# Where the attention mask is applied and who copies the state: VectorE, ScalarE and GpSimd in a chunked linear attention ahead of two feed-forward stages

## The chip, the cores and the metric

The kernel runs on one core of one Trainium2 chip. The metric is the device time of one execution in microseconds (us), lower is better. The engines are called as the profile calls them: PE is TensorE (PEld its weight loads), DVE is VectorE, ACT is ScalarE, POOL is GpSimd, SP is SyncE, which here only issues DMAs.

## The reference

Three stages follow each other. The first is a linear attention with decay, over 4 batches, 8 heads, 768 steps and a head dimension of 48:

```
for t in range(S):
    state = alpha[:, :, t, :, None] * state + np.einsum('bhd,bhe->bhde', k[:, :, t], v[:, :, t])
    y[:, :, t] = np.einsum('bhd,bhde->bhe', q[:, :, t], state)
```

Its output, 3072 tokens of 384 numbers, goes through a mixture of 8 experts with one expert for each token (384 to 1024 to 384, ReLU, scaled by two gates), and that through a dense stage (384 to 2048 to 384, squared ReLU). Everything is float32.

## The kernel before

The attention is done in 24 chunks of 128 steps, 6 for each batch. A chunk holds all 8 heads as 4 pairs (NP) of two halves a = 0 and 1; a half sits on partitions 64a to 64a + 47. For each chunk i:

- `decay(i)`: PE transposes alpha (`tr`, L268), ACT copies it out (`al`, L288, and its first column `a`, L291), DVE makes suffix and prefix products with two scans (`sp`, L294 and L303).
- `scaled(i)`: PE transposes k and q, and DVE multiplies them by the products as it takes them from PSUM (`kh`, `qh`, L318).
- `scores(i)`: PE multiplies `kh` with `qh` into two PSUM tiles `sc`, one for each half (L337). Then the causal mask is put on them: the tiles `m`. The two halves go different ways, and the change is here.
- `khat(i)` and `update(i)`: `kh` is transposed back (`khp`, L365), copied by ACT (`khn`, L367), and multiplied with v (`u`, L378). DVE adds the old state and multiplies by the decay (`st`, L383 or L385 and L387), and the new state is copied twice, once for each half, into the diagonal blocks of a zeroed tile `both` (L391). This copy is the other place of the change. It happens for chunks 0 to 4 of each batch, 20 times in all.
- `outputs(i)`: PE adds `both` times `qh` (L400) and `m` times v (L404) in PSUM tile `y`, ACT copies it to `yt` (L409).
- `rows(i)`, `logits(i)`: PE turns `yt` into token rows and gate logits (`fx`, L425), ACT copies the rows (`xn`, L435), DVE reduces the logits (`lg`, L442).

The chunks are pipelined by hand: iteration i of the loop at L770 writes out `scores(i+1)`, `scaled(i+2)`, `rows(i-1)`, `logits(i-1)`, `decay(i+3)`, `khat(i+1)`, `outputs(i)`, `update(i+1)`. So `m` and `both` of a chunk are needed by PE about one iteration after they are asked for. Every engine takes its instructions in the order written; waits are by semaphores.

Between these, small routing steps for groups of finished chunks are slipped into DVE's stream (`pulse`, a step or two at a time), and finished rows are scaled by ACT or DVE (`xn`, L574 and L572) and sent to their expert's place in memory by a scatter that POOL issues (`xs`, L129, after a tiny memset, L128). From chunk 19 on, the experts' weights are fetched and split in two parts by `parts`: ACT casts (L170), then POOL or, in the last iteration of the loop, DVE subtracts (both L171). The routing step `rk` (L503) of the last group of three chunks waits for DVE at the end of the attention. Behind that come the experts and the dense stage, which are matmuls of PE almost without a break.

Of the kernel before, what the change touches and what calls it, by code (L numbers as in the profile page):

```python
# [9 lines left out]
F32 = mybir.dt.float32  # L10
# [4 lines left out]
ALU = mybir.AluOpType  # L15
# [12 lines left out]
def moe_block_kernel(ctx: ExitStack, tc: tile.TileContext, q, k, v, alpha, w_gate, w_ogate,  # L28
                     w1, w2, w_in, w_out, out, dbg=None):
    nc = tc.nc  # L30
# [4 lines left out]
    P = 128  # L35
    NP = H // 2
# [29 lines left out]
    a1 = att.enter_context(tc.tile_pool(name="a1", bufs=1))  # L66

    with tc.manual_schedule():
# [7 lines left out]
        nc.scalar.activation(spare, ones[:, 0:1], AF.Exp)  # L76
        ident = const.tile([P, P], F32, name="ident")
        make_identity(nc, ident)
        mask = a1.tile([P, P], F32, name="mask")
        nc.gpsimd.memset(mask, 1.0)  # L80
        nc.gpsimd.affine_select(out=mask, in_=mask, pattern=[[1, P]], compare_op=ALU.is_ge,
                                fill=0.0, base=0, channel_multiplier=-1)
        tri = const.tile([P, P], BF16, name="tri")
        nc.gpsimd.memset(tri, 1.0)
        nc.gpsimd.affine_select(out=tri, in_=tri, pattern=[[1, P]], compare_op=ALU.is_gt,
                                fill=0.0, base=0, channel_multiplier=-1)
# [157 lines left out]
        both = []  # L244
# [85 lines left out]
        def scores(i):  # L330
            if i >= NCH:
                return
            ps = [p_sc.tile([P, NP, P], F32, tag="sc", name="sc") for _ in range(2)]
            for pr in range(NP):
                for a in range(2):
                    r = slice(64 * a, 64 * a + D)
                    nc.tensor.matmul(ps[a][:, pr, :], kh[i][r, pr, :], qh[i][r, pr, :],  # L337
                                     start=True, stop=True)

            held = [(gi, ranks(gi)) for gi in list(routing) if gi in waited or gi >= PICK - 1]  # L340
            waited.update(routing)
            for a in range(2):
                m = ms_p.tile([P, NP, P], F32, tag="m", name="m")
                if a == 0 and i > 0:
                    nc.vector.tensor_tensor(out=m, in0=ps[a],
                                            in1=mask.unsqueeze(1).to_broadcast([P, NP, P]),
                                            op=ALU.mult)
                else:
                    nc.scalar.copy(m, ps[a])
                    nc.gpsimd.affine_select(out=m, in_=m, pattern=[[0, NP], [1, P]],  # L350
                                            compare_op=ALU.is_ge, fill=0.0, base=0,
                                            channel_multiplier=-1)
                msk[i, a] = m
            for gi, ps in held:
                place(gi, ps)

        def has_next(i):
            return i < NCH and (i + 1) % NC != 0
# [11 lines left out]
        def update(i):  # L370
            if not has_next(i):
                return
            t = khn.pop(i)
            vt = slot("v", i)
            ps = p_1.tile([P, NP, D], F32, tag="ku", name="u")
            for pr in range(NP):
                for a in range(2):
                    nc.tensor.matmul(ps[64 * a:64 * a + 64, pr, :], t[:, pr, 64 * a:64 * a + 64],  # L378
                                     vt[:, 2 * pr + a, 0:D], start=True, stop=True)
            s = a3.tile([P, NP, D], F32, tag="st", name="st")  # L380
            pb = pend[i + 1].unsqueeze(2).to_broadcast([P, NP, D])
            if i % NC == 0:
                nc.vector.tensor_tensor(out=s, in0=ps, in1=pb, op=ALU.mult)  # L383
            else:
                nc.vector.tensor_tensor(out=s, in0=ps, in1=st[i], op=ALU.add)  # L385
                pulse()
                nc.vector.tensor_tensor(out=s, in0=s, in1=pb, op=ALU.mult)  # L387
            st[i + 1] = s
            for a in range(2):
                r = slice(64 * a, 64 * a + D)  # L390
                nc.scalar.copy(both[(i + 1) % 2][r, :, r], s[r])  # L391
            pulse()

        def outputs(i):
# [103 lines left out]
        def ranks(gi):  # L498
            n, g0 = GROUPS[gi], gstart[gi]
            s8 = [P, n, E]  # L500
            oh = onehot[:, g0:g0 + n, :]
            ps = psum(n)
            nc.tensor.matmul(ps, tri, oh, start=True, stop=False)  # L503
            nc.tensor.matmul(ps, ones, tot[:, gi:gi + 1, :].to_broadcast(s8), start=False,
                             stop=(n == 1))
            for c in range(n - 1):
                nc.tensor.matmul(ps[:, c + 1:, :], ones,
                                 oh[:, c:c + 1, :].to_broadcast([P, n - 1 - c, E]), start=False,
                                 stop=(c == n - 2))
            return ps  # L510
# [246 lines left out]
        for w, o in ((w_gate, XW), (w_ogate, XW + E)):  # L757
            for a in range(2):
                nc.sync.dma_start(
                    out=wx[64 * a:64 * a + D, :, o:o + E],  # L760
                    in_=w.rearrange("(pr a d) e -> a d pr e", a=2, d=D)[a])
# [38 lines left out]
        i = NCH - 2  # L800
# [9 lines left out]
        i = NCH - 1  # L810
# [223 lines left out]
        for n in range(NU):  # L1034
# [20 lines left out]
            if n:  # L1055
                down1(*last)
                m = n + NRA - 1 + sum(n < x for x in pauses)
# [13 lines left out]
            if n % 2 and n >= NU - 2 * NCH:  # L1071
                i = (n - NU + 2 * NCH) // 2
# [326 lines left out]
```

## Time and profile before

| | before |
|---|---|
| median of 3 runs | 815.82 us (815.4 to 816.51) |
| the profiled execution | 819.47 us |
| its span on the core | 817.5 us |
| PE busy in the span | 98% |
| DVE, ACT, POOL busy | 63%, 47%, 28% |
| attention | from the start to about 170 us |

Busy shares are means over the whole span; the attention is its first fifth, and the change touches nothing behind it. The profile gives one execution, whose own time is 3.65 us above the median of the runs, so a sum is made against the profiled execution and carried over to the median as a difference.

### The profile page before, as it was taken

The numbers are of one execution on the slowest core, as the hardware profiler recorded it, in microseconds if no ns is written. First come the engines' busy times: TensorE is split into PE (matmuls) and PEld (weight loads), VectorE is DVE, ScalarE is ACT, GpSimd is POOL, SyncE is SP. The second block draws the span as 40 slices with busy tenths as digits, with TensorE's granted clock in tenths as the row PEclk, the third lists the DMA queues.
The fourth block names the chain that finished last, engine by engine and source line by source line (L and its number), as shares of the span: only waits on it lengthen the run. The fifth ranks groups of instructions, "written<-read, shape, count | busy, mean of one in ns | idle before, by whom it ended". The sixth has DMA issues, their size and how long they took to land.

```text
span 817.5 us, 14112 instructions
## 1 busy us (share of the span) xinstructions
PE 798.3 (98%) x5215; PEld 735.1 (90%) x5215; DVE 515.8 (63%) x969; ACT 381.6 (47%) x734; POOL 230.1 (28%) x275
## 2 busy tenths in 40 slices
PE   9999999899999999999999999999999999999995
PEld 6999998788999999999988999999999999999995
DVE  8889998867568875897777677443343333333331
ACT  3777776564554555556444443333232333333221
POOL 3102341637447666777500000220001002002002
PEclk9999999899999999999999999999999999999998
DMA  9998994535455656675411010010000000000001
GB/s 144 171 215 180 209 176 93 194 122 159 137 160 157 181 132 192 181 171 170 79 40 59 20 58 21 39 40 1 0 4 36 1 1 39 1 1 40 1 0 43
DMA packets 153860, 74.98 MB, mean 92 GB/s; under 512 B 105406, under 2 KB 149430, under 8 KB 153782
## 3 DMA queue, kind: packets, MB, share of 16 engines
q1 hardware_dynamic: 149878, 64.52, 35.3%
q0 software_dynamic: 3904, 9.47, 3.2%
q8 instruction: 43, 0.70, 0.4%
q14 instruction: 35, 0.29, 0.2%
HBM read 61.76 MB, written 12.20 MB: 90 GB/s over the span
## 4 chain that ended last, share of the span: by engine, by line
PE 59%; issue 31%; DVE 4%; POOL 3%; ACT 2%; DMA 0%; SPq 0%; POOLq 0%; ACTq 0%; DVEq 0%
PE ha L1336 7%; PE ha L1338 7%; PE ha L1337 7%; PE acc L1336 7%; PE acc L1337 7%; PE acc L1338 7%; PE tr L268 4%; PE fx L425 3%; PE sc L337 3%; PE y L404 2%; POOL out_dram L129 2%; PE y L400 2%; PE tx L902 1%; PE u L378 1%; DVE sp L303 1%
## 5 line engine op out<-in xcount | busy, mean ns | idle before, releaser
L1336 PE MATMUL ha<-xh,w 128*128 128x512 f32 (+7 forms) x456 | 173.2, 380 | 0.0
L1338 PE MATMUL ha<-xh,w 128*128 128x512 f32 (+7 forms) x456 | 172.2, 378 | 0.0
L1337 PE MATMUL ha<-xl,w 128*128 128x512 f32 (+7 forms) x456 | 171.8, 377 | 0.0
L929 DVE SCALAR_TENSOR_TENSOR r<-ha,r 128x512 f32<-128x512 f32 x96 | 66.2, 690 | 141.5 <-ACT r L928 139.4
L171 POOL TENSOR_TENSOR w<-raw,w 128x768 fp32r<-128x768 f32 x60 | 114.3, 1904 | 74.6 <-ACT w L170 73.6
L928 ACT ACTIVATE r<-ha 128x512 f32<-128x512 f32 x96 | 57.4, 598 | 159.5 <-PE ha L1338 154.6
L129 POOL DMA_INDIRECT out_dram<-o,ids x24 | 24.5, 1021 | 378.1 <-ACT o L954 353.9
L1338 PE MATMUL acc<-w,hl 128*128 128x384 f32 x384 | 129.7, 338 | 0.0
L1337 PE MATMUL acc<-w,hh 128*128 128x384 f32 x384 | 129.7, 338 | 0.0
L1336 PE MATMUL acc<-w,hh 128*128 128x384 f32 x384 | 129.7, 338 | 0.0
L934 DVE TENSOR_TENSOR hl<-r,hh 128x512 fp32r<-128x512 f32 x96 | 66.7, 694 | 66.3 <-ACT hh L933 47.1
L933 ACT CAST hh<-r 128x512 fp32r<-128x512 f32 x96 | 59.5, 619 | 89.1 <-DVE r L929 87.8
L1338 PEld LDWEIGHTS ha<-xh,w 128*128 128x128 f32 x456 | 85.7, 188 | 14.0
L1337 PEld LDWEIGHTS ha<-xl,w 128*128 128x128 f32 x456 | 85.6, 188 | 10.1 <-DVE xl L905 0.2
L1336 PEld LDWEIGHTS ha<-xh,w 128*128 128x128 f32 x456 | 85.6, 188 | 9.3
L170 ACT CAST w<-raw 128x768 fp32r<-128x768 f32 x64 | 53.5, 836 | 57.8 <-PE acc L1338 42.2
L1336 PEld LDWEIGHTS acc<-w,hh 128*128 128x128 f32 x384 | 72.2, 188 | 4.1
L1337 PEld LDWEIGHTS acc<-w,hh 128*128 128x128 f32 x384 | 72.1, 188 | 3.9
L1338 PEld LDWEIGHTS acc<-w,hl 128*128 128x128 f32 x384 | 72.1, 188 | 0.0
L1336 PE MATMUL acc<-hh,w 128*128 128x448 f32 (+7 forms) x174 | 61.4, 353 | 0.0
L1337 PE MATMUL acc<-hl,w 128*128 128x448 f32 (+7 forms) x174 | 60.8, 350 | 0.0
L1338 PE MATMUL acc<-hh,w 128*128 128x448 f32 (+7 forms) x174 | 60.7, 349 | 0.0
(215 smaller groups left out, 1322.1 us busy)
## 6 DMA issues: line engine op xcount, KB each, us to landing
raw<-in_moe_w_dram SPq DMA_DIRECT2D x128, 192.0 KB
bits<-in_moe_w_in_dram SPq DMA_DIRECT2D x16, 384.0 KB
bits<-in_moe_w_out_dram SPq DMA_DIRECT2D x16, 384.0 KB
nat_al<-in_alpha_dram SPq DMA_DIRECT2D x24, 192.0 KB
nat_k<-in_k_dram SPq DMA_DIRECT2D x24, 192.0 KB
nat_q<-in_q_dram SPq DMA_DIRECT2D x24, 192.0 KB
nat_v<-in_v_dram SPq DMA_DIRECT2D x24, 192.0 KB
gx<-xs SPq DMA_DIRECT2D x22, 192.0 KB
```

What stands on the lines that cost most here:

```text
L129: ins = nc.gpsimd.indirect_dma_start(out=dst[:, :], out_offset=bass.IndirectOffsetOnAxis(ap=ix, axis=0), in_=src, in_offset=None)
L170: nc.scalar.copy(w[:, 0::2, :], raw)
L171: engine.tensor_tensor(out=w[:, 1::2, :], in0=raw, in1=w[:, 0::2, :].bitcast(F32), op=ALU.subtract)
L268: nc.tensor.transpose(ps[:, pr, :], src[:, pr, :], ident)
L337: nc.tensor.matmul(ps[a][:, pr, :], kh[i][r, pr, :], qh[i][r, pr, :], start=True, stop=True)
L928: nc.scalar.activation(r, ps, AF.Relu)
L929: nc.vector.scalar_tensor_tensor(out=r, in0=ps, scalar=0.0, in1=r, op0=ALU.max, op1=ALU.mult)
L933: nc.scalar.copy(hh, r)
L934: nc.vector.tensor_tensor(out=hl, in0=r, in1=hh.bitcast(F32), op=ALU.subtract)
L1336: nc.tensor.matmul(ps, st[0], mv[0], start=start, stop=False)
L1337: nc.tensor.matmul(ps, st[0], mv[1], start=False, stop=False)
L1338: nc.tensor.matmul(ps, st[1], mv[0], start=False, stop=stop)
```

## The change

Both halves of every chunk now get their mask in the way that one half had: ACT copies the scores from PSUM to `m`, and POOL's `affine_select` sets what lies below the diagonal to zero, in place. Before, half a = 0 of chunks 1 to 23 was masked by one DVE multiplication with a constant tile `mask`; the tile and the two POOL instructions that make it are gone. And the 40 copies of the state into `both` move from ACT to POOL.

```
-        mask = a1.tile([P, P], F32, name="mask")
-        nc.gpsimd.memset(mask, 1.0)
-        nc.gpsimd.affine_select(out=mask, in_=mask, pattern=[[1, P]], compare_op=ALU.is_ge,
-                                fill=0.0, base=0, channel_multiplier=-1)
...
             for a in range(2):
                 m = ms_p.tile([P, NP, P], F32, tag="m", name="m")
-                if a == 0 and i > 0:
-                    nc.vector.tensor_tensor(out=m, in0=ps[a],
-                                            in1=mask.unsqueeze(1).to_broadcast([P, NP, P]),
-                                            op=ALU.mult)
-                else:
-                    nc.scalar.copy(m, ps[a])
-                    nc.gpsimd.affine_select(out=m, in_=m, pattern=[[0, NP], [1, P]],
-                                            compare_op=ALU.is_ge, fill=0.0, base=0,
-                                            channel_multiplier=-1)
+                nc.scalar.copy(m, ps[a])
+                nc.gpsimd.affine_select(out=m, in_=m, pattern=[[0, NP], [1, P]],
+                                        compare_op=ALU.is_ge, fill=0.0, base=0,
+                                        channel_multiplier=-1)
...
             for a in range(2):
                 r = slice(64 * a, 64 * a + D)
-                nc.scalar.copy(both[(i + 1) % 2][r, :, r], s[r])
+                nc.gpsimd.tensor_copy(both[(i + 1) % 2][r, :, r], s[r])
```

Four lines are gone above the mask and five in `scores`, so that the changed file's L340, L341, L382 and L167 are what L349, L350, L391 and L171 were. The order of ACT's instructions from the scores of chunk 0 to the output of chunk 0, before (numbers behind names are buffers):

```order
L349 COPY m<-sc 128x512 x2
L288 COPY al_178<-tr 128x4x127
L291 COPY a_299<-tr 128x4
L391 COPY both_188<-st 48x4x48 x2
L349 COPY m<-sc 128x512
L288 COPY al_182<-tr 128x4x127
L291 COPY a_358<-tr 128x4
L367 COPY khn<-khp 128x512
L409 COPY yt<-y 128x512
```

The same place on ACT with the change:

```order
L340 COPY m<-sc 128x512 x2
L284 COPY al_175<-tr 128x4x127
L287 COPY a_296<-tr 128x4
L340 COPY m<-sc 128x512 x2
L284 COPY al_179<-tr 128x4x127
L287 COPY a_356<-tr 128x4
L358 COPY khn<-khp 128x512
L400 COPY yt<-y 128x512
```

The two copies to `both` have left ACT's stream, and a second copy of scores stands where they were, so nothing on ACT stands behind the state `st` of DVE any more.

On POOL, at the end of the attention, from the last scatter of the loop to the last weight tile of the attention, before:

```order
L129 DMA xs<-xn,idx 24576x384
L171 TENSOR_TENSOR w<-raw,w 128x2x384
L350 AFFINE_SELECT m<-m 128x512 x2
L171 TENSOR_TENSOR w<-raw,w 128x2x384
L128 MEMSET apart 128x1
```

The same place on POOL with the change:

```order
L382 COPY both_183<-st 48x4x48 x2
L167 TENSOR_TENSOR w<-raw,w 128x2x384
L341 AFFINE_SELECT m<-m 128x512 x2
L382 COPY both_185<-st 48x4x48 x2
L341 AFFINE_SELECT m<-m 128x512 x2
L167 TENSOR_TENSOR w<-raw,w 128x2x384
L124 MEMSET apart 128x1
```

The two state copies of an update now stand ahead of the first weight tile, and each chunk has two selects where it had one (the two selects of the rows before belong to two chunks).

## Rows read from the trace of the kernel before

**Rows 1.** The page's busy time and share of each engine.
```profile
PE 798.3 (98%) x5215; PEld 735.1 (90%) x5215; DVE 515.8 (63%) x969; ACT 381.6 (47%) x734; POOL 230.1 (28%) x275
```
**Rows 2.** Stretches: length, busy time (count) by engine, granted clock, DMA share, GB/s.
```profile
20.00:30.00 10.00, 9.26 (x130) 8.54 (x127) 9.38 (x19) 7.41 (x17) 1.27 (x2) 1.00 1.26 163
60.00:70.00 10.00, 10.00 (x133) 9.48 (x132) 9.79 (x27) 7.36 (x18) 1.31 (x3) 1.00 0.99 191
130.00:140.00 10.00, 8.58 (x97) 8.18 (x94) 8.62 (x27) 5.38 (x14) 0.68 (x2) 0.83 0.11 20
150.00:160.00 10.00, 6.41 (x75) 5.89 (x73) 8.02 (x22) 5.92 (x13) 5.46 (x6) 0.85 0.74 253
```
**Rows 3.** Groups by line: busy us, mean ns; idle before, and what ended it.
```profile
L350 POOL TENSOR_SCALAR_AFFINE_SELECT m<-m 128x512 f32<-128x512 f32 x25 | 19.0, 761 | 83.5 <-ACT m L349 83.4
...
L345 DVE TENSOR_TENSOR m<-sc,mask 128x512 f32<-128x512 f32 x23 | 15.7, 682 | 1.1 <-PE fx L425 0.9 <-PE sc L337 0.2
L349 ACT COPY m<-sc 128x512 f32<-128x512 f32 x25 | 14.5, 583 | 3.1 <-PE sc L337 1.9 <-PE fx L425 0.7
...
L391 ACT COPY both<-st 48x192 f32<-48x192 f32 x40 | 14.0, 350 | 15.9 <-DVE st L387 11.0 <-DVE st L383 3.4 <-DVE st L385 1.0
```
**Rows 4.** The same view: a POOL instruction with few elements.
```profile
L234 POOL MEMSET nat_v<- 128x128 f32 x2 | 0.3, 201 | 0.0
```
**Rows 5.** Timeline at the second chunk: start, duration, engine; idle before in brackets.
```profile
16.09 1.62 PE L337 MATMUL sc<-qh,kh 48*128 48x128 f32 x16
...
18.57 0.60 PE L268 MATMUL tr<-ident,nat_al 128*128 128x128 f32 x4
...
18.94 0.73 ACT L391 COPY both<-st 48x192 f32<-48x192 f32 x2 [3.08 <-DVE st L383]
19.00 0.60 PE L365 MATMUL khp<-ident,kh 128*128 128x128 f32 x4
...
19.53 1.09 PE L404 MATMUL y<-m,nat_v 128*64 128x128 f32 x16
...
20.70 0.62 ACT L367 COPY khn<-khp 128x512 f32<-128x512 f32 x1
...
21.37 0.67 PE L378 MATMUL u<-nat_v,khn 128*64 128x48 f32 x16 [0.74 <-ACT khn L367]
```
**Rows 6.** The chain that ended last, as chunk 18 comes out.
```profile
126.82 0.89 PE fx L425 x8
...
127.74 0.49 ACT xn L435
...
128.84 1.22 DVE sp L294
```
**Rows 7.** Timeline of ACT in a late chunk, after the third routing group.
```profile
139.76 1.06 ACT L326 ACTIVATE sp<-sp 128x1024 f32<-128x1024 f32 x1
...
141.19 0.73 ACT L391 COPY both<-st 48x192 f32<-48x192 f32 x2 [0.27 <-DVE st L387]
141.94 1.12 ACT L574 ACTIVATE xn<-xn,g 128x384 f32<-128x384 f32 x2
...
143.81 0.59 ACT L288 COPY al<-tr 128x508 f32<-128x508 f32 x1
```
**Rows 8.** Timeline: DVE and POOL at work at once, and the last routing step's wait.
```profile
122.67 0.65 POOL L350 TENSOR_SCALAR_AFFINE_SELECT m<-m 128x512 f32<-128x512 f32 x1
...
122.86 1.56 DVE L294 TENSOR_TENSOR_SCAN sp<-al,ends 128x512 f32<-128x512 f32 x1
...
152.08 1.83 POOL L171 TENSOR_TENSOR w<-raw,w 128x768 fp32r<-128x768 f32 x1
152.19 2.54 DVE L171 TENSOR_TENSOR w<-raw,w 128x768 fp32r<-128x768 f32 x1 [1.13 <-ACT m L349]
...
154.79 1.25 DVE L171 TENSOR_TENSOR w<-raw,w 128x768 fp32r<-128x768 f32 x1
...
157.72 0.18 PE L503 MATMUL rk<-onehot,tri 128*128 128x24 bf16 x1 [2.37 <-DVE st L385]
```

## The prediction, made before the change was run

> **What bounds the kernel now.** I read the page's busy shares first: PE is busy for 98% of the span, DVE for 63%, ACT for 47%, POOL for 28% [rows 1]. That says that a microsecond taken from DVE or ACT is worth nothing by itself; it counts only where PE waits for them. The change ends with the attention, so I went through the attention in stretches of 10 us. In the middle, from about 22 to 130 us, PE is busy all the time at the full granted clock (10.00 of 10.00 us in 60 to 70) though DVE has 9.79 us of work there [rows 2]. PE is less than full in two places: at the start (9.26 of 10.00 us in 20 to 30) and near the end (8.58 in 130 to 140, 6.41 in 150 to 160, where the clock also falls to a mean of 0.83 and 0.85 of the higher level) [rows 2]. So there are three questions: what the start gains, whether the full middle stays full, and what the end does.
>
> **What the change moves.** DVE loses 23 multiplications of 682 ns, 15.7 us in all. ACT gains 23 copies of 583 ns (13.4 us) and loses 40 of 350 ns (14.0 us), so its busy time is about the same, but it also loses the 15.4 us in which it stood still for DVE's state (11.0 + 3.4 + 1.0) [rows 3]. POOL gains 23 selects and 40 small copies. A select that meets nothing takes 0.65 us [rows 8]; the group's mean of 761 ns holds some that were held up [rows 3]. A POOL copy of 48 x 192 float32 is not in the trace. From below it is bounded by a memset of 128 elements a partition, 201 ns [rows 4], from above by a select of 512, 0.65 us; 192 elements lie near the lower one, and I take 0.3 us, 0.6 us for the pair. POOL's added work is then 23 x 0.65 + 40 x 0.3 = 27 us, in an attention in which it is mostly idle: it sat 83.4 us before its selects waiting for ACT's copies [rows 3].
>
> **The start.** At the second chunk ACT's next instruction is the pair of copies to `both`, and it waits 3.08 us for the state. Behind it in ACT's stream stand the masked half's copy, alpha's copies and `khn`, and PE waits 0.74 us for `khn` before `u` [rows 5]. With the change nothing on ACT waits for the state. The two score copies can go when the scores are done, at 16.09 + 1.62 = 17.71, and end at 17.71 + 2 x 0.58 = 18.9. Alpha's transposes end at 18.57 + 0.60 = 19.17, its copies take some 0.8 us, so `khn` (whose transposes end at 19.60) can run from about 20.0 to 20.6. `u` then follows on PE directly behind L404, which ends at 19.53 + 1.09 = 20.62, instead of at 21.37. **Minus 0.74 us**, with 0 and 0.74 as bounds. PE is the bound from there on, so the rest comes earlier by that.
>
> **The middle.** Nothing. PE has no idle time there that a faster DVE or ACT could give back. The new POOL work is covered: `m` and `both` are used an iteration later, some 6 us, and a chunk asks 2 x 0.65 + 0.6 = 1.9 us of POOL. If that cover failed, PE would wait at L400 or L404, and each wait would add its full length in every chunk. Toward the end the same holds while the chain goes PE `fx`, ACT `xn`, ACT `al`, DVE scan [rows 6]: `xn` starts when `fx` ends (126.82 + 0.89 = 127.71), whatever stood ahead of it on ACT.
>
> **One late chunk on ACT.** After the third routing group ACT does a square, waits 0.27 us for the state, does the pair of copies (0.73), then the scaling of two rows, the score copy, `xn` and `al` [rows 7]. The change takes away 0.27 + 0.73 and adds 0.58: at most minus 0.42 us. `xn` and `al` also wait for PE, so I take **minus 0.2 us**, with 0 as the other bound.
>
> **The last microseconds, where DVE and POOL meet.** At 152 us DVE and POOL both subtract a weight tile at L171. DVE's first one takes 2.54 us, its second 1.25; POOL's, started 0.11 us earlier, takes 1.83 [rows 8]. A scan next to a POOL select takes 1.56 us [rows 8] where it takes 1.22 alone [rows 6]. So one of the two holds the other up when both read from SBUF. DVE's second subtraction ends at 154.79 + 1.25 = 156.04; the routing steps behind it release `rk`, for which PE waits 2.37 us [rows 8], so what DVE loses here PE loses too.
>
> With the change the pair of state copies stands ahead of POOL's L171, by the order of its instructions. If POOL does them first, from 152.08 to 152.7, DVE's first subtraction runs until 153.9, POOL's then until 155.8, and DVE's second, behind it, until 157.0: 1.0 us later than before. If DVE goes first, at 152.19, it ends at 153.44, POOL's copies at 154.0, its subtraction at 155.9 and DVE's second at 157.1, again 1.0 us later. Only if DVE gets both through ahead of POOL does it gain, at most 2.54 - 1.25 = 1.29 us. On the other side the selects that now wait behind POOL's L171 come upon the routing steps, each worth up to 0.65 us. I take **plus 1.0 us**, with minus 1.29 and plus 2.3 as bounds.
>
> The Trainium skill (SBUF — State Buffer, "SBUF: two separate sides") says of this pair that it is "an exclusive lock, not a bandwidth split", for a DVE instruction with two SBUF inputs against a POOL instruction that reads SBUF: whichever starts first keeps the other out until its end. By that rule the order of arrival decides, and the added selects and copies can only bring more such meetings, which is the slower rival below; the sum would be the same. The trace agrees in kind, though not to the last tenth: POOL's row ends at 153.91, from where a free 1.25 us would end at 155.16, and DVE's row ends at 154.73.
>
> **Sum.** -0.74 - 0.2 + 1.0 = about +0.1 us on a profiled execution of 819.47 us; on the median of the runs, 815.82 us, which is 3.65 us lower, that is 815.9 us. What a measurement can tell from no change is 0.2%, 1.6 us, so the forecast is no change.
>
> **Rivals.**
> - *Faster, 0.22.* DVE gets its two subtractions through ahead of POOL's, as it has one instruction of 0.68 us less ahead of them and ACT's cast comes earlier without the wait for the state. Then -0.74 - 0.2 - 1.29 = -2.2 us, 813.6. For it: before, POOL was first by only 0.11 us. Against it: DVE's second one needs another cast of ACT first, and POOL stands ready by then. A shorter wait before `rk` could also spare some of the lowered clock, at most (1 - 0.85) x 10 = 1.5 us more, 812.1.
> - *Slower, 0.22.* The added POOL work holds up DVE in the last five chunks, where DVE and ACT set the pace: each select that meets a scan or a routing step of two SBUF inputs costs up to 0.65 us. Above the sum's +0.1 it takes three such meetings on the path to pass +1.6 us; three give +2.0, 817.8, five give +3.3, 819.1. For it: the held-up scan and the 2.54 us [rows 8]. Against it: the two selects come right behind the scores, before the scan has its alpha.
> - *DVE's whole 15.7 us come back, 0.02.* About 800 us. It would need PE to wait for DVE in the middle, and PE is full there [rows 2].
> - *The forecast, 0.54.*
>
> The range for 8 in 10 goes a little beyond the rivals' near ends: 813.6 to 818.0. Faster by over 0.2%: 0.22 + 0.02, less the part of the faster case that falls short of 1.6 us, 0.22. Slower: 0.22. Within: 0.56.
>
> **What would show it.** The profile after should have `u` of the second chunk at about 20.6 us, with no wait of PE before it, and 20 to 30 us full for PE. POOL's copy rows should be near 0.3 us. In the middle PE should stay at 10.00 of 10.00 us. At the end, DVE's second L171 and the wait before `rk` decide: the first ending about 0.1 us later than 156.04 if the early gains of 0.9 us and the loss of 1.0 cancel. I am wrong if PE shows waits at L400 or L404 in the middle, if a POOL copy costs near 0.65 us and stands before scatters that are then late, or if DVE's subtractions no longer meet POOL's.

## The result, and the profile after

The changed kernel takes 826.33 us (median of 6 runs, 824.32 to 831.15); the kernel before took 815.65 beside it (6 runs, 815.23 to 816.51). The ratio is 1.0134, 95% interval 1.0106 to 1.0162. Forecast were 815.9 us and a range up to 818.0: the change is slower, and by more than the range allowed.

The profiled execution of after took 826.52 us, with a span of 824.8 (before 819.47 and 817.5). Line numbers are those of the changed file: what was L350 is L341 (POOL's select), L391 is now L382 (the state's copy), L404 L395, L129 L125, L171 L167. The busy line of its page, to be held against [rows 1]:

```profile
PE 796.8 (97%) x5215; PEld 733.2 (89%) x5215; DVE 503.6 (61%) x946; ACT 377.9 (46%) x717; POOL 259.7 (31%) x336
```

DVE lost 12 us, ACT 4, POOL gained 30 (foreseen were 15.7, almost none and 27), and that says nothing of the loss. The stretches (length, then busy time of PE, PEld, DVE, ACT and POOL, granted clock, DMA share, GB/s) do, held against [rows 2]:

```profile
20.00:30.00 10.00, 7.37 (x97) 6.77 (x94) 6.85 (x15) 5.18 (x11) 2.57 (x5) 1.00 1.29 158
60.00:70.00 10.00, 10.00 (x127) 9.58 (x127) 9.70 (x28) 6.55 (x16) 3.81 (x8) 1.00 1.04 205
80.00:90.00 10.00, 6.38 (x70) 5.73 (x68) 8.23 (x15) 5.85 (x13) 3.08 (x4) 0.93 1.19 218
90.00:100.00 10.00, 9.57 (x88) 8.66 (x90) 1.99 (x5) 3.92 (x9) 7.82 (x15) 0.72 0.99 182
130.00:140.00 10.00, 7.85 (x82) 7.12 (x81) 4.52 (x9) 3.86 (x10) 7.82 (x12) 0.83 0.60 131
```

PE is full at 60 us as before, and then has a hole at 80 to 100 us, in the middle that I had called full. After it the granted clock is lower (a mean of 0.72 of the higher level from 90 to 100 us), so that PE runs at the lower one for part of the stretch. The stretch from 130 to 140 us was not full before either (8.58 us at 0.83 [rows 2]), but the two rows don't show the same thing: before, PE waited 1.42 us there for `rk`, at 132.60; in after that wait comes at 143.71, and the waits at 130 to 133 us are new ones, shown below. The groups say who was late; POOL's two, with the idle time ahead of them:

```profile
L341 POOL TENSOR_SCALAR_AFFINE_SELECT m<-m 128x512 f32<-128x512 f32 x48 | 34.7, 745 | 11.7 <-ACT m L340 10.5
...
L382 POOL COPY both<-st 48x192 f32<-48x192 f32 x40 | 14.6, 365 | 71.8 <-DVE st L378 42.2 <-DMA xs<-xn,idx 10.3 <-DVE st L374 7.4
```

A copy costs 365 ns, near the 0.3 us that I took. But 10.3 us of the wait ahead of the copies is for a DMA, `xs<-xn,idx`: the scatters that POOL itself issued. A copy of the state reads nothing that they write. POOL's timeline at the first hole (start, duration; idle before in brackets):

```profile
75.10 1.14 POOL L125 DMA_INDIRECT xs<-xn,idx  x1 [1.69 <-ACT a L287]
76.30 2.13 POOL L341 TENSOR_SCALAR_AFFINE_SELECT m<-m 128x512 f32<-128x512 f32 x2
78.38 0.09 POOL L124 MEMSET apart<- 128x1 f32 x1
83.16 1.63 POOL L125 DMA_INDIRECT xs<-xn,idx  x1 [4.69 <-DVE d L298]
84.79 0.12 POOL L124 MEMSET apart<- 128x1 f32 x1
85.10 0.97 POOL L125 DMA_INDIRECT xs<-xn,idx  x1 [0.19 <-issue]
86.07 0.35 POOL L382 COPY both<-st 48x192 f32<-48x192 f32 x1
90.03 0.34 POOL L382 COPY both<-st 48x192 f32<-48x192 f32 x1 [3.61 <-DMA xs<-xn,idx]
90.44 0.10 POOL L124 MEMSET apart<- 128x1 f32 x1
90.75 0.98 POOL L125 DMA_INDIRECT xs<-xn,idx  x1 [0.22 <-issue]
91.79 1.22 POOL L341 TENSOR_SCALAR_AFFINE_SELECT m<-m 128x512 f32<-128x512 f32 x2
```

The first copy of the pair, rows 0 to 47, runs at 86.07. DVE had the state much earlier, at 79.08 + 0.36 = 79.44:

```profile
79.08 0.36 DVE L378 TENSOR_TENSOR st<-st,pend 128x192 f32<-128x192 f32 x1
```

So this copy stood 6.6 us in POOL's queue, behind the two scatters at 83.16 and 85.10, of which the first had itself waited 4.69 us. PE could have used the state from 86.38, when its product before this one was done (85.78 + 0.60), so the queue alone used up nearly all of the 7 us in between. The second copy, rows 64 to 111, stands until 90.03, when the scatter issued at 85.10 has landed. PE needs both halves:

```profile
90.43 2.07 PE L391 MATMUL y<-qh,both 128*128 128x128 f32 x8 [4.05 <-POOL both L382]
92.48 2.34 PE L395 MATMUL y<-m,nat_v 128*64 128x128 f32 x15
```

These are the waits at L400 and L404 (now L391 and L395) by which I said that I should be wrong. Both products also take about twice as long as free ones (1.06 and 1.09 us): from 90.4 to 94.7 us the granted clock is 0.50, the lower level. The compiled program has the wait in it, at five of the twenty updates and only at the copy that begins at row 64; an update of the first burst (DMASW are landings of POOL's own DMAs):

```
70 L382 COPY both_185<-st 48x4x48 [waits DVE_49,PE_49]
71 L382 COPY both_185<-st 48x4x48 [waits DMASW1_49,DMASW2_49,DMASW0_49,Pool_49]
```

In the trace the five waits of POOL are 3.6, 1.2, 4.2, 1.3 and 4.2 us. The one of the second burst (the pair runs at 123.61 and 128.15, a wait of 4.18 us) costs PE no wait for `both`; PE waits for the masks, whose selects stand behind the late copy (129.91 us on POOL):

```profile
129.06 1.06 PE L391 MATMUL y<-qh,both 128*128 128x128 f32 x8
131.19 0.43 PE L395 MATMUL y<-m,nat_v 128*64 128x128 f32 x2 [1.07 <-POOL m L341]
132.70 1.45 PE L395 MATMUL y<-m,nat_v 128*64 128x128 f32 x13 [1.07 <-POOL apart L124]
```

At the end (161.15 and 166.43, 4.22 us put down to "issue") PE waits 0.29 us for `both` and 0.71 for `m`.

### The profile page after: what moved, and what is told of

Read it like the earlier page. It is cut to its first block, busy times and chain, and to the rows that moved or that the text cites. A ratio compares the mean times of both kernels' runs of the same rounds, so it can differ in the third digit from the quotient of the medians.

```text
span 824.8 us, 14196 instructions
## 1 busy us (share of the span) xinstructions
PE 796.8 (97%) x5215; PEld 733.2 (89%) x5215; DVE 503.6 (61%) x946; ACT 377.9 (46%) x717; POOL 259.7 (31%) x336
## 4 chain that ended last, share of the span: by engine, by line
PE 44%; issue 31%; POOL 3%; DVE 1%; DMA 0%; ACT 0%; SPq 0%; POOLq 0%; DVEq 0%; ACTq 0%
PE ha L1327 7%; PE ha L1328 7%; PE ha L1329 7%; PE acc L1327 7%; PE acc L1328 7%; PE acc L1329 7%; POOL out_dram L125 2%; PE tx L893 1%; PE y L395 0%; DVE okc L998 0%; DMA gx<-xs 0%; ACT sp L322 0%; POOL apart L124 0%; DVE o L941 0%; PE fx L416 0%
## 5 line engine op out<-in xcount | busy, mean ns | idle before, releaser
L125 POOL DMA_INDIRECT out_dram<-o,ids x24 | 24.4, 1015 | 380.0 <-ACT o L945 355.8
L167 POOL TENSOR_TENSOR w<-raw,w 128x768 fp32r<-128x768 f32 x60 | 114.4, 1907 | 73.2 <-ACT w L166 60.5
```

The costliest lines, as they stand in the source:

```text
L125: ins = nc.gpsimd.indirect_dma_start(out=dst[:, :], out_offset=bass.IndirectOffsetOnAxis(ap=ix, axis=0), in_=src, in_offset=None)
L167: engine.tensor_tensor(out=w[:, 1::2, :], in0=raw, in1=w[:, 0::2, :].bitcast(F32), op=ALU.subtract)
```

## The experiments

The runs were made on five chips, and on two of them the kernel before itself took 819.9 us with a wider spread. So ratios to the kernel before on the same chip are compared, not medians. (The ratio is the one on record; it can differ by up to 0.002 from the quotient of the two medians.)

| run | this, us | before there, us | ratio (95% interval) |
|---|---|---|---|
| c_after (the change) | 827.71 | 815.49 | 1.0141 (1.0126 to 1.0156) |
| c_before | 815.64 | 815.49 | 1.0001 (0.9989 to 1.0013) |
| e1_masks_alone | 824.81 | 819.93 | 1.0041 (1.0015 to 1.0066) |
| e2_copies_alone | 824.39 | 819.93 | 1.0045 (1.0019 to 1.0070) |
| e3_from_row_0 | 825.33 | 819.93 | 1.0049 (1.0024 to 1.0074) |
| e3_again | 826.79 | 819.85 | 1.0080 (1.0051 to 1.0110) |
| e4_upper_on_act | 826.65 | 819.93 | 1.0076 (1.0052 to 1.0099) |
| e5_one_scatter | 818.60 | 815.49 | 1.0040 (1.0027 to 1.0053) |
| e8_one_scatter_64 | 823.22 | 819.85 | 1.0046 (1.0021 to 1.0072) |
| e7_copies_on_dve | 821.78 | 819.85 | 1.0030 (1.0010 to 1.0051) |
| e9_dve_alpha_first | 822.88 | 819.85 | 1.0047 (1.0024 to 1.0069) |
| f1_until_14 | 818.82 | 815.89 | 1.0037 (1.0023 to 1.0050) |
| f2_from_15 | 818.43 | 815.89 | 1.0030 (1.0018 to 1.0043) |
| f3_idle_64 | 824.26 | 815.89 | 1.0110 (1.0095 to 1.0125) |
| f4_idle_0 | 820.19 | 815.89 | 1.0057 (1.0037 to 1.0078) |
| f5_state_behind | 835.23 | 818.16 | 1.0199 (1.0172 to 1.0225) |
| e6_alpha_first | 814.38 | 815.49 | 0.9988 (0.9979 to 0.9997) |
| f6_alpha_again | 817.64 | 818.16 | 0.9987 (0.9973 to 1.0000) |

The traces give a second measure. In each profile I took the start of the product `y<-m` of every chunk, subtracted the same start in c_before, and looked at how the difference grows from stage to stage (us; "end" is the first matmul of the experts). The first burst of scatters lies between chunks 10 and 13, the second between 16 and 18.

| profile | chunk 1 | 1 to 10 | 10 to 13 | 13 to 16 | 16 to 18 | 18 to end |
|---|---|---|---|---|---|---|
| before | -0.55 | 0.00 | 0.26 | 0.00 | 0.22 | 3.57 |
| c_after | 0.90 | -0.09 | 6.42 | -0.08 | 5.80 | -0.51 |
| after | 0.01 | -0.09 | 6.99 | -0.09 | 4.22 | -0.08 |
| e1 masks alone | 0.15 | 0.92 | 1.67 | 0.91 | 0.49 | 4.76 |
| e2 copies alone | 1.63 | 0.08 | 6.89 | -0.08 | 1.13 | -0.94 |
| e3, again | 0.41, -0.97 | 0.86, 0.64 | 2.83, 6.00 | 0.65, 0.63 | 0.00, 0.00 | 3.48, 3.66 |
| e4 upper on ACT | -0.84 | 0.11 | 5.38 | 0.11 | 0.00 | 4.31 |
| e5 one scatter, row 0 | -0.84 | 0.35 | -0.01 | 1.17 | 0.00 | 2.48 |
| e8 one scatter, row 64 | -0.79 | -0.09 | 0.13 | -0.09 | 0.00 | 4.26 |
| e7 copies on DVE | -1.02 | 0.38 | 0.94 | 0.55 | 0.10 | 3.09 |
| e9 copies on DVE, alpha first | -2.59 | 0.38 | 1.09 | 0.54 | 0.10 | 4.46 |
| f1 until chunk 14 | 1.18 | 1.01 | -0.02 | 0.83 | 0.03 | 1.54 |
| f2 from chunk 15 | -0.06 | 0.01 | -0.01 | -0.01 | 2.64 | 3.07 |
| f3 idle, row 64 | -0.18 | 0.02 | 5.84 | 0.00 | 1.59 | -1.32 |
| f4 idle, row 0 | -0.10 | 0.00 | 4.50 | 0.00 | 0.00 | 0.17 |
| f5 state behind | -1.02 | 8.49 | 0.66 | 3.07 | 1.24 | 8.61 |
| e6, f6 alpha first | -1.99, -2.14 | 0.00, 0.01 | 0.00, 1.61 | 0.00, 0.00 | 0.00, 0.19 | 0.00, 1.98 |

One profile is one execution: f6 shows 1.61 us in the first burst and 1.98 at the end where the same program shows 0.00 in e6, and before shows 3.57 at the end. Differences under 2 us in one profile, and under 4 at the end, are therefore no evidence by themselves.

**The change itself and the kernel before, on one chip.**

> The kernel before, profiled on the chip of the runs beside it, as their measure. Its median is its own by definition (ratio 1.000 within 0.002). For the start: if the clock of TensorE at 6 to 17 us differs from one execution to the next whatever the kernel, some profile of it shows the transposes at 7 to 17 us in 0.6 us a set of four and not 1.1 us, the second chunk's u before 20 us, and then a wait for the load of alpha near 22 to 25 us, as in the changed kernel; if the change made the start faster, the rows are as in rows 5.

> The changed kernel, on the same chip as the other runs of this group: 1.010 to 1.016 of before, with the copy for rows 64 to 111 waiting for scatters at five places and TensorE losing about 6 us between 81 and 99 us.

Both as expected. The change's 12.2 us of medians agree with the 12.44 us of its profile against c_before: 0.9 at the start, 6.4 and 5.8 in the two bursts. And c_before's start is not that of [rows 5]: its sets of four transposes take 0.60 to 0.67 us from 5.5 us on, where those of the first profile take 1.06 to 1.09 until 15 us (the granted clock reads 1.00 from 5 to 17 us in both), `u` of the second chunk is at 19.56, and then PE waits for the load of alpha, as in the changed kernel.

**The two parts apart.** The masks alone (copies left on ACT), then the copies alone (masks as before):

```
e1:  -  nc.gpsimd.tensor_copy(both[...][r, :, r], s[r])
     +  nc.scalar.copy(both[...][r, :, r], s[r])          # on the changed kernel
e2:  -  nc.scalar.copy(both[...][r, :, r], s[r])
     +  nc.gpsimd.tensor_copy(both[...][r, :, r], s[r])   # on the kernel before
```

> Masks of both halves by ScalarE's copy and GpSimd's select as in the change, the two copies of the state into the block-diagonal tile still on ScalarE. Theory A (the change lost its time because GpSimd's copy for rows 64 to 111 stands behind the landing of scatters issued before it): no instruction of GpSimd waits for a landing between 80 and 165 us, TensorE has no wait above 1 us for the block-diagonal tile, and the time is 812 to 817 us. Theory B (the masks cost it: 24 more selects of 745 ns on GpSimd and 24 more copies on ScalarE make the mask tiles late): the second product of y waits for selects as in the change, and the time is 820 us or more.

> Only the two copies of the state go to GpSimd; masks as in the kernel before. Theory A: the copy for rows 64 to 111 waits for scatters at five places again, TensorE waits about 4 us for the block-diagonal tile near 86 us and about 1 us later on, and the time is 822 to 829 us, because the gains of a lighter VectorE are missing too. Theory B: 40 copies of 0.35 us hurt nobody without the added selects, and the time is 814 to 818 us.

Neither theory had it right: on a kernel before of 815.65 us the two ratios are 819.0 and 819.3 us, between A and B in both runs. Each part alone costs 0.4%, together they cost 1.4%. With the masks alone PE never waits for POOL; ACT is late instead, in nine places (in c_before in two, 2.4 us). From the waits of PE (in total, times, longest):

```profile
PE u L369 <- ACT khn L358: 6.2, 9, 2.1
```

That fits ACT being short of the time that the state's copies would have left free. The copies alone lose 6.9 us in the first burst, with the landing wait, and only 1.1 in the second.

**The same work without the landing wait.** In e3 the second half is written by a select that begins at row 0; in e4 it goes to ACT. In neither does the program wait for scatters.

```
e3:  nc.gpsimd.tensor_copy(t[0:D, :, 0:D], s[0:D])
     nc.gpsimd.affine_select(out=t[0:64 + D, :, 64:64 + D], in_=s[0:64 + D], pattern=[[0, NP], [0, D]],
                             compare_op=ALU.is_ge, fill=0.0, base=-64, channel_multiplier=1)
e4:  (nc.scalar.copy if a else nc.gpsimd.tensor_copy)(both[...][r, :, r], s[r])
```

> The change, but the second half of the state goes into the block-diagonal tile by a GpSimd select that begins at row 0 (rows 0 to 111, keeping rows 64 up) in place of a copy that begins at row 64. Same engine, same order, a little more work; the compiled program has no wait for scatters at it. Theory A: no wait for a landing, TensorE has no wait above 1 us for the block-diagonal tile, time 812 to 818 us. Theory B (GpSimd is simply too busy, or is held off by VectorE, when the state is ready): the block-diagonal tile is as late as in the change, time 822 us or more. Theory C (a smaller version of B: the second instruction costs some 0.5 us at every update): 818 to 822 us.

> The version whose second half begins at row 0 once more, since the chip of its first run gave the kernel before 819.9 us and these chips 815.5. If the ratio of the first run (1.0049) is right, 1.003 to 1.007 of before, so that the wait for landings is worth two thirds of the loss (1.0141). If that chip was at fault, 1.008 or more.

> The change, with the copy for rows 64 to 111 on ScalarE and the one for rows 0 to 47 on GpSimd. Theory A: GpSimd's copy for rows 0 to 47 never waits for scatters, so the time is 812 to 817 us. Theory B: GpSimd still has the 24 more selects and half of the copies, and the time stays at 820 us or more.

The loss of the second burst is gone (5.80 and 4.22 against 0.00 in all three profiles). The loss of the first is not (2.83, 6.00, 5.38): selects and scatters are late there without any landing wait. In e3 PE waits 1.28 and 1.07 us for masks, in its repetition 1.26 and 1.07; the pair of selects that finishes those masks takes 2.97 us in e3, beside two scans of DVE, where a free pair takes 1.22, so the slower selects may have a part in it. The 2.83 and the 6.00 are one program; the granted clock from 90 to 100 us was 1.00 in the one profile and 0.66 in the other. And the ratios say the same: two fifths to two thirds of the loss went. So theory A holds for the second burst and is not enough for the first. By time none of the three is in A's range (on 815.65 us they are 819.6, 822.2 and 821.8 us); e3's first is in C's, but its loss is not spread over the updates as C has it. The repetition's 1.0080 lies on the very bound at which I would have blamed the first chip, and it ran on a chip like that one (before 819.85), so "two thirds of the loss" is not confirmed.

**One scatter at a time.** On e3 and on the change, the second and third of the loop's three places for scatters are skipped in the first 18 iterations:

```
             if i < NCH - 3:
                 check(i)
-            move(pace)
+            if pace > 1:
+                move(pace)
             update(i + 1)
-            move(pace)
+            if pace > 1:
+                move(pace)
```

> The version whose second half begins at row 0, with at most one scatter in each iteration of the first 18 (up to three before), so that GpSimd's queue holds one scatter, two writes of the state and two selects in an iteration. Theory Q (what is left of the loss there is GpSimd's queue: the selects of the mask and the state stand behind three scatters of 1.0 to 1.6 us): the waits of TensorE for mask tiles at 88 to 92 us (2.4 us) go, and the time is 1.000 to 1.004 of before. Theory L (the selects are late because VectorE's scans hold GpSimd off: 2.97 us for two in place of 1.22): they stay late, and the time is 1.004 to 1.008 of before.

> The change with its copy from row 64 on GpSimd, but with at most one scatter in each iteration of the first 18. The program now has nine copies that wait for a landing (five in the change), most for one scatter that was issued some 4 us earlier. If the price of a landing is the 4.2 us from issue to landing less what lies between issue and copy, most of these waits are under 1 us, and the time is 1.004 to 1.008 of before, 0 to 3 us above the one-scatter version that begins at row 0. If every such wait costs as those of the change (1 to 4 us), it is 1.014 or more.

Both bursts cost nothing now, with the landing wait (e8: 0.13 and 0.00) and without it (e5: -0.01 and 0.00). That is theory Q: what was late stood behind a burst. It is the bursts that tell Q from L here, not the time: 1.0040 lies on the bound between them. Some pairs of selects are still slow in e5 (2.13 us at 80.48, beside a scan), and PE waits for none of them. The landing waits of e8 are not the short ones that I expected. The scatter is issued right ahead of the pair of copies, not 4 us earlier, and in the iterations with one scatter POOL waits 2.3 to 3.8 us each time. They cost PE nothing because the copies still end 1.5 us or more before PE needs them; POOL, and then PE, at the first of them:

```profile
79.14 1.14 POOL L125 DMA_INDIRECT xs<-xn,idx  x1 [5.34 <-DMA nat_q<-in_q_dram]
83.32 0.48 POOL L382 COPY both<-st 48x192 f32<-48x192 f32 x1 [2.68 <-DMA xs<-xn,idx]
85.42 1.06 PE L391 MATMUL y<-qh,both 128*128 128x128 f32 x8
```

**Neither POOL nor ACT copies the state.** On the changed kernel `nc.vector.tensor_copy` in place of `nc.gpsimd.tensor_copy`:

> The masks as in the change, both copies of the state on VectorE, which the change relieved of 15.7 us of masks; neither GpSimd nor ScalarE has them. Theory Q+A (two separate costs: GpSimd's queue of scatters, state and selects, and ScalarE's queue where it has both the added mask copies and the state): TensorE waits neither for mask tiles at 86 to 92 us nor for khn (in the version with the masks alone 6.2 us in nine places), time 0.999 to 1.004 of before. Theory M (the masks on ScalarE and GpSimd cost it by themselves, wherever the state is copied): waits for mask tiles or khn stay, 1.004 to 1.009.

1.0030, inside Q+A: 0.94 us in the first burst, with the bursts as they were, and `khn` late in two places (1.7 us), as often as in c_before, where e1 had nine. The selects alone, two for each chunk, do not suffer much from the bursts; the state does.

**A copy that nobody reads.** The kernel before, with one small POOL copy more per update, from row 64 (f3) or from row 0 (f4):

```
f3:  +  nc.gpsimd.tensor_copy(blank[64:112, 0:4], s[64:112, :, 0])
f4:  +  nc.gpsimd.tensor_copy(blank[0:48, 0:4], s[0:48, :, 0])
```

> The kernel before with one more small GpSimd copy per update (48 rows, 4 elements each, from row 64 of the state into a tile that nobody reads). The program makes it wait for landings at five places. If such a wait hurts only through what stands behind it in GpSimd's queue: selects of one half of the mask come 1 to 4 us later there, TensorE waits for mask tiles up to 3 us in all, 1.001 to 1.005 of before. If a landing wait stops more than the queue: 1.006 or more. If the selects have slack enough: within 0.001.

> The control of the run with the idle copy from row 64: the same copy from row 0 (rows 0 to 47), which the program doesn't make wait for landings. It still stands in GpSimd's queue until VectorE has the state. If a wait for the state in GpSimd's queue costs nothing by itself: within 0.001 of before. If it does (scatters and selects stand behind it): 1.001 to 1.004, and the row-64 version more.

A telling pair, and both lost more than I had allowed for a wait that only holds up POOL's queue (1.005 for f3, 1.004 for f4). An instruction of 0.2 us whose result is never used costs 0.57%, and 1.10% if it also waits for landings: the landing wait is worth 0.5%, and the added instruction without it as much. In f4 the whole loss is one event of 4.5 us, in the first burst. What is late is the one mask half that POOL selects there; PE's wait in f3, and then in f4 (timelines of the two kernels):

```profile
91.41 1.75 PE L406 MATMUL y<-m,nat_v 128*64 128x128 f32 x13 [3.85 <-POOL apart L129]
```
```profile
90.14 1.75 PE L406 MATMUL y<-m,nat_v 128*64 128x128 f32 x13 [2.52 <-POOL apart L129]
```

The releaser is named `apart`, the tiny memset that follows the select. In f3 the way there is plain: the idle copy stands for a landing, and the select (90.72 us) comes behind it, with a memset and a scatter in between.

```profile
88.89 0.48 POOL L393 COPY blank<-st 48x4 f32<-48x4 f32 x1 [3.45 <-DMA xs<-xn,idx]
```

How far the idle copy of f4 can be followed is seen on POOL and in SP's queue. In c_before, the first scatter of the burst, the last clearing of the experts' memory, the second scatter, and the select that PE needs:

```profile
74.66 1.12 POOL L129 DMA_INDIRECT xs<-xn,idx  x1 [5.73 <-DMA nat_q<-in_q_dram]
...
77.90 0.58 SPq L673 DMA_DIRECT2D xs<-zero  x1
...
82.09 1.75 POOL L129 DMA_INDIRECT xs<-xn,idx  x1 [4.67 <-DVE lg L442]
...
86.58 0.64 POOL L350 TENSOR_SCALAR_AFFINE_SELECT m<-m 128x512 f32<-128x512 f32 x1
```

and in f4:

```profile
72.98 0.18 POOL L393 COPY blank<-st 48x4 f32<-48x4 f32 x1 [4.17 <-DVE st L388]
...
73.11 0.09 POOL L129 MEMSET apart<- 128x1 f32 x1
...
77.37 1.92 POOL L130 DMA_INDIRECT xs<-xn,idx  x1 [4.17 <-issue]
...
80.90 0.58 SPq L675 DMA_DIRECT2D xs<-zero  x1
...
85.12 0.98 POOL L130 DMA_INDIRECT xs<-xn,idx  x1 [5.12 <-DVE xn L574]
...
89.36 0.73 POOL L351 TENSOR_SCALAR_AFFINE_SELECT m<-m 128x512 f32<-128x512 f32 x1
```

The clearing waits for the first scatter to land (issued at 77.90, 3.2 us behind 74.66; at 80.90, 3.5 us behind 77.37), and by the program the second scatter waits for the clearing (82.09 and 85.12: 4.2 us behind it both times). With the idle copy, the first scatter comes 2.7 us later, the second 3.0 later, and the select behind the burst 2.8 later. From the first scatter on the delay is handed down the queue. Why the first scatter is late is not shown: the copy's wait for the state is over at 72.98, before c_before's first scatter ran (74.66), the rows to be sent were scaled by 74.4 and 74.3 us, and the profile shows no releaser for the time until 77.37. In f3, behind the same wait (until 72.91), the first scatter runs at 75.04. So the pair does not show that the wait for the state costs the 0.57%, only that the added copy does.

**The state behind the scatters.** e3 with both writes moved from `update` to the start of the next iteration, behind the last scatter:

```
         for i in range(NCH - 2):
             pace = 1 if i < gstart[PICK] else 3
+            widen(i)        # the two writes of e3
             scores(i + 1)
```

> The version whose second half begins at row 0, with both writes of the state moved behind the last scatter of their iteration, ahead of the next chunk's selects; scatters in bursts as before, same instructions. Most of the writes now need no wait for VectorE at all. Theory H (an instruction that waits for the state holds up scatters and selects that could run): the loss between chunk 10 and chunk 13 falls from 2.8 and 6.0 us (the two profiles of that version) to under 1.5 us, time 1.002 to 1.005 of before. Theory W (three scatters, two selects and two writes are simply too much for GpSimd between two chunks): the state itself comes behind the scatters and TensorE waits for it, loss there 3 us or more, 1.006 or more.

By its time, 1.0199, the worst of all, theory H falls. The 0.66 us between chunks 10 and 13 are what H asked for, but the loss has only moved one chunk ahead: chunk 10 itself comes 7.4 us late against chunk 9 (inside the 8.49 of the table), and PE waits 13.5 us for the state in six places, as W has it. Ahead of the burst the state's write holds the scatters and selects up; behind it the state is late itself. PE's longest wait there:

```profile
86.96 2.08 PE L397 MATMUL y<-qh,both 128*128 128x128 f32 x8 [6.17 <-POOL both L387]
```

**The start.** The loads of two chunks of v behind `decay(1)`, so that the fifth load of alpha is issued earlier; on the kernel before (twice), and on e7:

```
-        load("v", 2)
-        load("v", 3)
         decay(1)
+        load("v", 2)
+        load("v", 3)
```

> The kernel before with the loads of the third and fourth chunk's v issued behind decay(1) and not ahead of it, so that the fifth load of alpha is issued about 2.4 us earlier (18.4 us, not 20.8). If the load of alpha ends the wait of a fast start: 0.5 to 2 us less than before (0.9975 to 0.9995). If the start of the kernel before is bound by TensorE itself, as rows 5 show it: within 0.001 of before.

> The kernel before with the two loads of v behind decay(1), a second time. 0.997 to 0.9995 of before if the first result (0.9988) holds.

> The version with both copies on VectorE, with the two loads of v behind decay(1) as well. In the kernel before that move was worth 2.0 us in the profiles and 1.1 us in the medians. If the start is bound by the load of alpha in both, 1 to 2 us under the version without the move; if it beats the kernel before, 0.997 to 0.9995 of it.

In c_before, and then in e6, the transposes of that alpha:

```profile
25.38 0.66 PE L268 MATMUL tr<-ident,nat_al 128*128 128x128 f32 x4 [2.15 <-DMA nat_al<-in_alpha_dram]
```
```profile
23.44 0.60 PE L268 MATMUL tr<-ident,nat_al 128*128 128x128 f32 x4
```

The start is bound by the load: 2.0 us in the profiles, 1.1 and 0.5 us in the medians. e6 is the one version under both kernels, on one chip below 1 with its whole interval, on the other up to it. On e7 the same move brought chunk 1 forward by 1.6 us, but the end gave it back (4.45 us there against 3.09), and the ratio is not better: a miss.

**Where the rest sits.** The new arrangement for chunks 0 to 14 alone (state by e3's writes, the first group's scatters one per iteration), or from chunk 15 on alone (the change as it is):

```
f1:  -                if a == 0 and i > 0:
     +                if a == 0 and i > 0 and i >= 15:
     ...
     +            if i + 1 < 15:
     +                nc.gpsimd.tensor_copy(t[0:D, :, 0:D], s[0:D])
     ...
f2:  -                if a == 0 and i > 0:
     +                if a == 0 and i > 0 and i < 15:
     ...
     +                copy = nc.gpsimd.tensor_copy if i + 1 >= 15 else nc.scalar.copy
```

> The new arrangement for chunks 0 to 14 only (masks by ScalarE and GpSimd, state by GpSimd from row 0, one scatter per iteration as long as the first group lasts), the arrangement of the kernel before from chunk 15 on. Theory D (with the burst of scatters spread, what is left of the loss sits in the last chunks, where ScalarE has the mask copies beside its other work): 0.998 to 1.002 of before. Theory E (the added copies on ScalarE cost a little in every chunk): 1.002 to 1.005.

> The kernel before for chunks 0 to 14, the change as it is from chunk 15 on (masks by ScalarE and GpSimd, both state copies on GpSimd, one from row 64, scatters as before). Theory D: the second landing wait (4.2 us at 124 us in the change) and the last chunks cost 3 to 7 us, 1.004 to 1.009 of before, with no loss ahead of 110 us. Theory E: no more than half of the 1.014 of the change sits here; 1.002 to 1.004.

1.0037 and 1.0030: both times lie in E's ranges, and f1 is outside D's. But E's reason, a little in every chunk, does not fit f2, which loses nothing until chunk 16 and then 2.64 us behind the landing wait of the second burst. Why f1, with both bursts free, keeps 0.37% is not settled: its profile lost 1.2 us by chunk 1, 1.0 by chunk 10, 0.8 behind chunk 13 and 1.5 at the end, in no one place.

## Why the prediction was wrong

**The step that failed** is "The middle. Nothing." with its ground: "The new POOL work is covered: `m` and `both` are used an iteration later, some 6 us, and a chunk asks 2 x 0.65 + 0.6 = 1.9 us of POOL." The 1.9 us were right (a pair of selects 1.22 us when free, a pair of copies 0.74). The cover was there, too: 7 us between the state (79.44) and PE's need of it (86.38) in the first burst of after. What I left out is that POOL takes its instructions in order, and what stands between them there: up to three scatters in an iteration, about 1 us each and each with a wait for its rows or for a landing. An instruction that waits holds up all that stand behind it. The first copy of that pair stood 6.6 us behind two scatters, the second 3.6 us more for a landing, and PE waited 4.05 us. Nor did every chunk pay, as I had it for a cover that fails: PE stood in the bursts and at the end. Busy time covers an instruction; it does not cover a queue. Shown by that timeline, by e5 and e8 (one scatter at a time, no loss in either burst, though e8's landing waits are 2.3 to 3.8 us) and by f5 (behind the scatters the state is later still). f3 and f4 show that even an idle copy in that queue costs 1.10% and 0.57%.

**A wait that the diff doesn't show.** The landing wait of the copy from row 64 is in none of my steps and none of my rivals. Shown by e3 and e4 against the change in the second burst (0.00 against 4.2 and 5.8 us), and by f3 against f4 (0.5%). I had read the order of POOL's instructions before predicting, but without their waits, where it stands.

**The sign that I named.** "If a POOL copy costs near 0.65 us and stands before scatters that are then late" was half of the truth: the cost was 0.365, and the scatters were late all the same, because the copy waits.

**The start** (-0.74 us) was not confirmed. `u` of the second chunk did come earlier (19.13 in after), but PE then waited 2.63 us for alpha, and chunk 1's mask product began at 27.30, 0.56 us later than in the profile before. The step "PE is the bound from there on" failed: the load is (c_before, e6). And the start of [rows 5] was slow because PE's products took about twice as long until 15 us (1.06 to 1.09 us for four transposes, against 0.60 to 0.67 in c_before) in that one execution: in c_before the same kernel starts as after does. That a lower clock did it is not shown, since the granted clock reads 1.00 there in both.

**The late chunk on ACT** (-0.2 us) is too small to be found beside these.

**The end** (+1.0 us by DVE and POOL at L171 at once) did not appear in the change, because POOL stood still for a landing just there; DVE's two subtractions ran free, and PE's wait before `rk` fell from 2.37 us to 1.60:

```profile
161.06 0.96 DVE L167 TENSOR_TENSOR w<-raw,w 128x768 fp32r<-128x768 f32 x1 [1.54 <-ACT w L166]
161.15 1.06 POOL L382 COPY both<-st 48x192 f32<-48x192 f32 x1
...
162.66 0.96 DVE L167 TENSOR_TENSOR w<-raw,w 128x768 fp32r<-128x768 f32 x1 [0.51 <-ACT w L166]
...
165.31 0.17 PE L494 MATMUL rk<-onehot,tri 128*128 128x24 bf16 x1 [1.60 <-DVE st L376]
...
166.43 0.34 POOL L382 COPY both<-st 48x192 f32<-48x192 f32 x1 [4.22 <-issue]
```

So DVE's free subtraction takes 0.96 us; the 1.25 that I took for it had a select of POOL beside it. In e5, without that wait, the meeting is there: DVE's two take 0.96 + 4.03 = 4.99 us where c_before's took 2.54 + 1.25, 1.2 us more where I took 1.0, and `rk` waits 4.89 us against 2.88.

```profile
152.17 0.96 DVE L167 TENSOR_TENSOR w<-raw,w 128x768 fp32r<-128x768 f32 x1 [0.53 <-ACT w L166]
...
153.77 4.03 DVE L167 TENSOR_TENSOR w<-raw,w 128x768 fp32r<-128x768 f32 x1 [0.51 <-ACT w L166]
153.98 0.35 POOL L381 COPY both<-st 48x192 f32<-48x192 f32 x1
...
154.61 1.79 POOL L167 TENSOR_TENSOR w<-raw,w 128x768 fp32r<-128x768 f32 x1
```

The Trainium skill (SBUF — State Buffer, "SBUF: two separate sides") has it that a DVE instruction with two SBUF inputs and a POOL instruction that reads SBUF shut each other out, and that the first to start goes on to its end. 0.96 us free and 4.03 us beside POOL agree with the first part. The second does not show: DVE's row starts at 153.77, POOL's writes and its subtraction run from 153.98 to 156.40 (POOL's spans are rough), and DVE ends at 157.80.

**The slower rival** had the sign and, in the main, the wrong mechanism: selects that meet DVE's scans do take longer (two in 2.97 us in e3, 1.22 free), but with one scatter at a time PE lost nothing between chunks 10 and 13. The faster rivals were far off.

**Open.** Between 0.3 and 0.5% stay in every version with part of the new arrangement (e5, e7, e8, f1, f2). By the profiles of e5, e7 and e8 most of it lies behind chunk 18, where the kernel before itself differs by 3.6 us between its two profiles, so the traces can't place it. Why f4's first scatter is late is open as well. What decides whether the clock falls after a short wait (e3 and its repetition) is not known either. And why the program makes the copy from row 64 wait, and no copy from row 0, was not found out.

## What to carry to other kernels

Before an instruction is moved to an engine that issues DMAs, list what stands around it in that engine's queue in the busiest iteration, with the waits of each as compiled: the price is the waits in that queue, less the time until the result is needed, and not the instruction's own time. Where PE needs a result within the iteration, keep it out of a queue that issues bursts, or spread the bursts, here one scatter in an iteration. And try one cheap idle copy on the receiving engine first: f3's lost 1.1% and f4's 0.6%, where the change lost 1.4%.

## What the runs showed of the hardware that I had not expected

A POOL copy that begins at row 64 waited for landings of scatters in the program as compiled, the same copy from row 0 did not; a scatter took 4.2 us from issue to landing (median of 24 in after). A wait of PE costs more than its length: in the change 4.05 us of waiting became 6.99 us of loss between chunks 10 and 13, above all since the two products behind it took 2.07 and 2.34 us at a granted clock of 0.50, where free ones take 1.06 and 1.09. And a start with faster products gains nothing by itself: c_before was 1.85 us ahead of the first profile at chunk 0 and 0.55 us behind it at chunk 1, waiting for a load.
